# Weight addresses held in TensorE registers, and the batch order found by matmuls, in an attention and mixture-of-experts kernel

## The chip, the cores and the metric

The kernel runs on one core of a Trainium2 chip. The metric is the device time of one launch in microseconds, the median of several runs; lower is better. The profile is of one execution and counts from the start of its span.

## The reference

Two stages follow each other. The first is attention between 512 tokens x and 32 state rows, for 8 batches of 8 heads of width 64, in both directions:

```
scores = x @ state.T / 8 ;  xread = softmax(scores) @ state      # 512 rows a batch
scores2 = state @ x.T / 8 ; sread = softmax(scores2) @ x         # 32 rows a batch
rows = concatenate([xread, sread]) with the heads side by side   # 8 * 544 = 4352 rows of 512
```

The second is a mixture of 8 experts without dropping. Each row goes to the expert with the largest of its eight logits:

```
logits = rows @ w_gate ;  e = argmax(logits) ;  gate = softmax(logits)[e]
y = gate * (relu(rows @ w1[e]) @ w2[e])          # w1: 512 x 1024, w2: 1024 x 512, per expert
```

## The kernel before

**One expert a batch.** The kernel guesses the expert of each batch from the sums of its state rows, and lets all 512 token rows of the batch go through that one expert. The 256 state rows (32 a batch) are routed one batch at a time: each group of 32 rows has its own guess. At the end a flag says whether every row's true argmax was the guessed one; if not, a slow path under `tc.If` computes again. With the inputs of this study it isn't entered.

**Weights in slots.** The weights of all experts have a place in SBUF, `wt`, 8 slots of 16,384 fp16 values a partition: half 0 of a slot is w1, half 1 is w2. GpSimd loads them (`load_w`, with a cast from fp32 on the way), in the order in which the batches first need their expert: slot 0 is the expert of batch 0, and so on. Until they are loaded, parts of slots 6 and 7 serve as scratch and as two of the three buffers for x. So which slot a batch uses is known at run time only. The batch order is worked out on VectorE, on one partition (`guess_first` for batch 0, `guess_rest`, `guess_rest2` and `full_order` for the others), and leaves the loads' order in `ordi` and a word with three bits per batch in `slotw`. TensorE loads that word into a register (`slot_of`, line 437) and takes the batch's three bits (`field`, line 427).

**The letters.** The order on every engine is written out by hand, as strings of short names that `run` executes in turn. The ones used below, per batch: C casts x to fp16, T and X transpose it; N gives the scores `sn`, E, I and J their exponentials in two fp16 halves; S and F the scores the other way; G the gate logits, R, U, V, P and A the normalised attention `aT`; Z, z, t and u the state rows' reading into `sx`; M, g and h the gate. The token rows never become a 512 x 512 matrix: W multiplies the state by w1 (`sw`, copied to `SW` by K), L multiplies `SW` by `aT` (`hps`), H applies relu into `hT`, Q multiplies by w2 (`yps`, eight matmuls for each of four row groups), Y scales by the gate and O stores. Batch k's L, H, Q and Y run between the steps of batch k+1's attention (prefix `+`) and batch k+2's loading (`++`). `STEP` is the pattern of batches 3 to 6, `LATE` that of the first three.

**W.** For each of two halves fh of the hidden width, W issues eight matmuls of 64 rows by 32 columns, in eight places of the array (`pinned`, line 230), into two banks. K copies one bank each to `SW`. Three banks (`psm`) are shared by W, L and the tail's `hs`.

**The tail.** After the last batch the state rows of all batches are computed. s0 to s9 find their experts, in two groups g of 4 batches: each of the 32-row blocks j has a slot of its own, and the rows that don't agree with their block's main expert go through a third pass, p = 2, with a side (which of the groups) for each block. Pass p is l (`hs`: 32 matmuls of 128x32, four side by side), m (relu), n and o (transposes), q (`ys`, 32 matmuls) and y (scaling). v compares all token rows' choices with the guesses, w sums that into the flag with a matmul, r stores. The tail's order, at the end of the string for the last batch:

```
Q0 Y0a s3 s4 s5 s6 s7 s8 s9
l20 m20a l21 m21v Q1 Y1v O0
n2 o2v l00 m00a l01 m01a v w
q2 y2a n0 o0v
Q2 Y2a l10 m10a l11 m11v
q0 y0a r0 n1 o1v
Q3 Y3a O1
q1 y1a r1
```

s6 (line 594) loads two words into TensorE registers and takes sixteen fields out of them. Every matmul that reads `wt` at a run-time slot is written with a dynamic slice; the address is then computed by a register instruction ahead of each of these matmuls.

Of the kernel before, what the change touches and what calls it, by code (L numbers as in the profile page):

```python
# [19 lines left out]
B = 8  # L20
# [9 lines left out]
FAR = 1.0e6  # L30


def _consts():
# [3 lines left out]
        "bone": p[:, None] // 32 == np.arange(4)[None],  # L37
        "rev": np.broadcast_to(8 - np.arange(E), (128, E)),
        "pw": np.broadcast_to(2.0 ** (8 - np.arange(B)), (128, B)),
        "io": np.broadcast_to(np.arange(8), (128, 8)),  # L40
        "oct": np.broadcast_to(8.0 ** np.arange(B), (128, B)),
# [11 lines left out]
    )  # L53
    c = {
# [16 lines left out]
def kernel(  # L71
# [53 lines left out]
    posv = sb([1, E], FP32, "posv")  # L125
    hone = sb([1, B, E], FP32, "hone")
    ordi = sb([1, E + 1], I32, "ordi")
    slotw = sb([1, 1], I32, "slotw")
    vrow = sb([1, 2, E], FP16, "vrow")
# [13 lines left out]
    bone, rev, pw, io, octw = (const(1, n) for n in ("bone", "rev", "pw", "io", "oct"))  # L143
# [25 lines left out]
    zm = scr(256).rearrange("p (b e c) -> p b e c", b=B, e=E)  # L169
    zz = scr(64)  # L170
    hv = scr(256)
# [33 lines left out]
    def load_w(i, half, at=None):  # L205
        if ("w", i) not in order:
            at = i if at is None else at
            order["w", i] = P_.value_load(
                ordi[:, at : at + 1], min_val=0, max_val=E - 1
            )  # L210
        rv = order["w", i]
        if half == 0:
            s = moe_w1[ds(rv, 1)].rearrange("o (c l) f -> l (o c) f", l=128)
        else:
            s = moe_w2[ds(rv, 1)].rearrange("o (c l r) f -> l (o c) (r f)", l=128, r=2)
        ins = P_.dma_start(  # L216
            out=wt[:, i, half].rearrange("p (c f) -> p c f", c=4), in_=s
        ).ins
        tc.declare_no_dep(ins, group="wmm", reason="readers of slots filled before")
        tc.add_to_no_dep_group("w", ins)  # L220
        wloads[half].append(ins)
# [8 lines left out]
    def pinned(out, lhsT, rhs, pos, size, start, stop):  # L230
        def sym(ap, **k):
# [3 lines left out]

        name = (
# [7 lines left out]
            ins=[sym(rhs), sym(lhsT, for_matmul_weights=True)],  # L244
# [182 lines left out]
    def field(word, shift, mask):  # L427
        t = nc.tensor
        r = t.alloc_register(f"fld{len(order)}")
        order["fld", len(order)] = r  # L430
        if shift:
            t.reg_alu(r, word, shift, OP.logical_shift_right)
            t.reg_alu(r, r, mask, OP.bitwise_and)
        else:
            t.reg_alu(r, word, mask, OP.bitwise_and)
        return t.snap(r, min_val=0, max_val=mask)

    def slot_of(d):
        if "slot" not in d:
            if d["b"] == 0:  # L440
                d["slot"] = 0
            else:
# [4 lines left out]
                d["slot"] = field(order["word"], 3 * d["b"], 7)  # L447
        return d["slot"]

    def op_W(d, fh):  # L450
        slot = slot_of(d)
        d["sw", fh] = [bank([128, 512], FP32, "sw", psm) for _ in range(2)]
        for c in range(4):
            for r in range(2):
                rows = slice(64 * r, 64 * r + 64)
                i = pinned(
                    d["sw", fh][r][32 * c : 32 * c + 32],
                    d["bd"][rows, c, 32 * r : 32 * r + 32],
                    w1(slot, rows, c, fh * 512, fh * 512 + 512),
# [3 lines left out]
                    True,  # L463
                )
                if "loop" not in d and d["b"]:
                    first = fh == 0 and c == 0
# [25 lines left out]
    def op_Q(d, q):  # L492
        slot = slot_of(d)
        ps = d["yp", q] = bank([128, 512], FP32, "yps", psy)
        for f in range(8):
            i = mm(
                ps, hT[:, f, q * 128 : q * 128 + 128], w2(slot, f), f == 0, f == 7
            ).ins
            if "loop" not in d and d["b"]:
                dyn(i, wloads[1][: d["b"] + 1] if q == 0 and f == 0 else ())  # L500
# [93 lines left out]
    def op_s6(_):  # L594
        w = [
            nc.tensor.value_load(g_["swi"][:, k : k + 1], min_val=0, max_val=m)
            for k, m in ((0, 2**24 - 1), (1, 2**24 - 1))
        ]
        g_["slots"] = [
            [field(w[0], 12 * g + 3 * j, 7) for j in range(4)] for g in range(2)  # L600
        ] + [[field(w[1], 5 * j, 7) for j in range(4)]]
        g_["side"] = [field(w[1], 5 * j + 3, 1) for j in range(4)]
# [52 lines left out]
    def lhs_state(p, j, c, t=0):  # L655
        if p < 2:
            return sx[:, t, c, p, j, :]
        return sx[:, t, c, ds(g_["side"][j], 1), j, :].rearrange("p o n -> p (o n)")

    def op_l(_, p, fh):  # L660
        ps = g_["hs", p, fh] = bank([128, 512], FP32, "hs", psm)
        for c in range(4):
            for j in range(4):
# [3 lines left out]
                    w1(g_["slots"][p][j], slice(0, 128), c, fh * 512, fh * 512 + 512),  # L667
# [3 lines left out]
                    c == 3,  # L671
                )
                dyn(i, wloads[0] if c == 0 and fh == 0 and j == 0 else ())
# [23 lines left out]
    def op_q(_, p):  # L697
        ps = g_["ys", p] = bank([128, 512], FP32, "ys", psy)
        for f in range(8):
            for j in range(4):  # L700
# [3 lines left out]
                    w2(g_["slots"][p][j], f),  # L704
# [3 lines left out]
                    f == 7,  # L708
                )
                dyn(i, wloads[1] if f == 0 and j == 0 else ())  # L710

    def op_y(_, p, e):
        if p == 2:
            yS = g_["yS"] = sb([128, 2, DM], FP32, "ysb", 3)
            sd = g_["sdm"] = sb([128, 2], FP32, "sdm")
            V_.tensor_copy(sd, g_["gm"][:, 1])
            for g in range(2):
                scale(e, yS[:, g], g_["ys", 2], sd[:, g : g + 1])
            return
        if "yM" not in g_:  # L720
            g_["yM"] = sb([128, 2, DM], FP32, "ysb", 3)
        V_.scalar_tensor_tensor(
            g_["yM"][:, p],
            g_["ys", p],
            g_["gm"][:, 0, p : p + 1],
            g_["yS"][:, p],
            op0=OP.mult,
            op1=OP.add,
        )
# [10 lines left out]
    def run(table, k=0, ctx_=None):  # L740
        for w in table.split():
# [15 lines left out]
            elif n in "svwlmnoqyr" or n[0] == "s":  # L757
# [22 lines left out]
    A_.dma_start(kt[1][0], kt[1][1])  # L780
    state_first(nc.sync, 0)
    state_first(nc.sync, 1)
    A_.dma_start(wgr, moe_w_gate.rearrange("(c r) e -> r c e", r=128))
    A_.dma_start(kt[0][0], kt[0][1])
    load_x(0, nc.sync, 0, 4)
    load_x(0, nc.sync, 4, 8)
    for c in range(4):
        for r in range(2):
            state_dma(nc.sync, c, r)
    A_.dma_start(kt[2][0], kt[2][1])  # L790

    V_.memset(ones, 1.0)
    V_.memset(one32, 1.0)
    V_.memset(hT[:, 0], 0.0)
    scratch(V_.memset(wgx, 0.0))
    warm = sb([1, 1], FP32, "warm")
    V_.memset(warm, 0.0)
    A_.activation(warm, warm, AF.Exp)
    P_.memset(bd[:, 0], 0.0)
    P_.memset(bd[:, 1:B], 0.0)  # L800

# [44 lines left out]
    hrow = lambda k: hv[0:1, 64 * k : 64 * k + 64].rearrange("p (b e) -> p b e", e=E)  # L846
    mrow, krow = hv[0:1, 192:200], hv[0:1, 200:208]
    m8 = sb([1, 8], FP32, "m8")
    i8 = sb([1, 8], U32, "i8")

    def guess_first():
# [7 lines left out]
        h0 = sb([1, E], FP32, "h0")  # L859
        V_.tensor_copy(h0, hp)  # L860
        V_.max(m8, h0)
        V_.max_index(i8, m8, h0)
        V_.tensor_copy(ordi[:, E : E + 1], i8[:, 0:1])
        f0 = sb([1, 1], FP32, "f0")
        V_.tensor_copy(f0, i8[:, 0:1])
        V_.tensor_scalar(hone[:, 0], io[0:1], f0, None, op0=OP.is_equal)

    def guess_rest():
        sp = bank([128, 7, 4], FP32, "sp")
        for b in range(1, B):  # L870
            mm(sp[:, b - 1], stl[:, b, :], bone)
        wv = bc(wgr.rearrange("p c e -> p e c"), 1, 7)
        scratch(V_.tensor_tensor(zm[:, 1:B], bc(sp, 2, E), wv, op=OP.mult))
        scratch(V_.reduce_sum(zz[:, 8:64].rearrange("p (b e) -> p b e", e=E), zm[:, 1:B], axis=AX_X))

    def guess_rest2():
        hp = bank([1, 7, E], FP32, "hp7")
        mm(hp.rearrange("p b e -> p (b e)"), one32, zz[:, 8:64])
        h0 = hrow(0)[:, 1:B]
        mx = mrow[:, 1:B]  # L880
        scratch(V_.reduce_max(mx, hp, axis=AX_X))
        scratch(V_.tensor_tensor(h0, hp, bc(mx, 2, E), op=OP.is_equal))
        scratch(V_.tensor_tensor(h0, h0, bc(rev[0:1], 1, 7), op=OP.mult))
        scratch(V_.reduce_max(mx, h0, axis=AX_X))
        V_.tensor_tensor(hone[:, 1:B], bc(rev[0:1], 1, 7), bc(mx, 2, E), op=OP.is_equal)

    def full_order():
        h0, h1 = hrow(0), hrow(1)
        key = krow
        scratch(V_.tensor_tensor(h0, hone, bc(pw[0:1], 2, E), op=OP.mult))  # L890
        scratch(V_.reduce_sum(key, h0.rearrange("p b e -> p e b"), axis=AX_X))
        scratch(
            V_.scalar_tensor_tensor(key, key, 16.0, rev[0:1], op0=OP.mult, op1=OP.add)
        )
        scratch(V_.tensor_tensor(h1, bc(key, 1, E), bc(key, 2, E), op=OP.is_gt))
        V_.reduce_sum(posv, h1, axis=AX_X)
        scratch(
            V_.tensor_tensor(h0, bc(posv, 1, E), bc(io[0:1], 2, E), op=OP.is_equal)
        )
        scratch(V_.tensor_tensor(h0, h0, bc(io[0:1], 1, E), op=OP.mult))  # L900
        with nc.allow_low_precision(reason="small whole numbers"):
            V_.reduce_sum(ordi[:, 0:E], h0, axis=AX_X)

    def slot_word():
        h0, h1 = hrow(0), hrow(1)
        scratch(V_.tensor_tensor(h1, hone, bc(posv, 1, B), op=OP.mult))
        scratch(V_.tensor_tensor(h0, h1, bc(octw[0:1], 2, E), op=OP.mult))
        with nc.allow_low_precision(reason="whole numbers below 2 to the 24"):
            V_.reduce_sum(slotw, h0.rearrange("p b e -> p (b e)"), axis=AX_X)

    def codes():
        h0 = hrow(0)
# [243 lines left out]
```

## Time and profile before

| | |
|---|---|
| median of three runs | 225.24 us (222.94 to 226.63) |
| span of the profiled execution | 219.3 us |
| TensorE busy | 188.3 us, 86% |
| VectorE, ScalarE, GpSimd busy | 116.9, 87.0, 33.6 us |
| token matmuls `yps`, 256 | 60.0 us, 379 ns each as recorded, overlapping |
| state matmuls `hs` and `ys`, 96 each | 8% and 6% of the chain that ended last |
| `sw`, 128 | 8% of that chain |
| weight loads, 16 | 1024 KB each, 20.4 us from issue to landing (median) |

The page's busy share is an average over four stretches with different limits: the start until W of batch 0 (22.6 us), the way to W of batch 1 (54.4), six steps until W of batch 7 (157.7), and the tail. [...] so the pace is read from the distance of starts.

### The profile page before, as it was taken

Reading aid. Unit: us, or ns where it says so; the run is one execution under the profiler, and the core shown is the slowest. Engines: PE = TensorE matmul, PEld = TensorE weight load, DVE = VectorE, ACT = ScalarE, POOL = GpSimd, SP = SyncE. Lnnn points to the kernel's source line nnn. Section 1 sums busy time; section 2 is a strip of 40 time slices with the busy share of each in tenths; the row PEclk is TensorE's granted clock in tenths of the full one; section 3 lists DMA queues with packets and bytes.
Section 4 is the critical chain, followed back from the end, with each engine's and each line's share of the span. In section 5 each row is a group of like instructions: output and inputs, shape, how many; then the busy total and the mean of one; then the engine's idle time right before and its main releaser. Section 6 shows DMA issues by size and latency. Waiting matters only on the chain.

```text
span 219.3 us, 5315 instructions
## 1 busy us (share of the span) xinstructions
PE 188.3 (86%) x1934; PEld 99.2 (45%) x1935; DVE 116.9 (53%) x307; ACT 87.0 (40%) x170; POOL 33.6 (15%) x42
## 2 busy tenths in 40 slices
PE   5654767879999899899999999999997099999990
PEld 2244334545445445435545555554543022565650
DVE  1655466987578378476566566567567200611211
ACT  3260337604462571564475467368162101114010
POOL 3501000914300710460130022100000000000000
PEclk9996788999999999999999999999999979999997
DMA  5999800799999999999999955892202000200042
GB/s 112 233 229 274 256 5 0 119 211 275 290 205 298 263 250 295 257 279 275 253 221 247 302 199 92 204 185 99 100 13 83 0 3 0 84 17 0 3 144 57
DMA packets 17268, 35.26 MB, mean 161 GB/s; under 512 B 3800, under 2 KB 4952, under 8 KB 17240
## 3 DMA queue, kind: packets, MB, share of 16 engines
q0 software_dynamic: 10352, 24.12, 51.2%
q1 hardware_dynamic: 5736, 10.23, 13.6%
q10 hardware_dynamic: 1152, 0.53, 1.0%
q8 instruction: 19, 0.31, 0.6%
q14 instruction: 9, 0.07, 0.1%
HBM read 42.73 MB, written 8.91 MB: 236 GB/s over the span
## 4 chain that ended last, share of the span: by engine, by line
PE 78%; DVE 10%; ACT 4%; issue 3%; DMA 1%; SPq 0%; DVEq 0%; ACTq 0%
PE yps L86 25%; PE hps L86 13%; PE hs L252 8%; PE sw L252 8%; PE ys L252 6%; PE sr L86 4%; PE xtp L282 2%; PE lgp L86 2%; PE wp L86 1%; ACT xT L97 1%; PE sn L86 1%; DVE enlo L310 1%; PE ss L86 1%; DMA wt<-in_state_dram 1%; PE gp L86 1%
## 5 line engine op out<-in xcount | busy, mean ns | idle before, releaser
L86 PE MATMUL yps<-wt,hT 128*128 (+1 forms) x256 | 60.0, 379 | 0.0
L86 PEld LDWEIGHTS <-hT 128*128 128x128 f16 x256 | 24.2, 99 | 26.1 <-issue 1.6
L86 PE MATMUL hps<-aT,SW 128*128 128x512 f16 x128 | 33.2, 393 | 3.0 <-DVE hT L487 3.0
L504 ACT ACTIVATE ysb<-yps,gall 128x512 f32<-128x512 f32 x21 | 14.4, 687 | 31.8 <-PE yps L86 31.4
L487 DVE TENSOR_SCALAR hT<-hps 128x512 f16<-128x512 f32 x34 | 22.8, 689 | 7.2 <-PE hps L86 7.2
L252 PE MATMUL hs<-wt,sx 128*32 x96 | 18.5, 395 | 5.4 <-issue 5.2
L485 ACT ACTIVATE hT<-hps 128x512 f16<-128x512 f32 x30 | 17.8, 597 | 9.7 <-PE hps L86 9.1
L252 PE MATMUL sw<-wt,bd 64*32 (+1 forms) x128 | 19.1, 404 | 2.4 <-ACT SW L97 2.2
L86 PEld LDWEIGHTS <-SW 128*128 128x128 f16 x128 | 11.8, 99 | 19.5 <-issue 9.7
L97 ACT CAST SW<-sw 128x512 f16<-128x512 f32 x20 | 11.3, 588 | 21.0 <-PE sw L252 21.0
L216 POOL DMA_DIRECT2D wt<-in_moe_w_dram x16 | 12.2, 766 | 33.5 <-DVE sx L423 20.0
L252 PEld LDWEIGHTS <-sx 128*32 128x32 f16 (+1 forms) x96 | 6.8, 94 | 16.3 <-issue 14.4
L364 DVE TENSOR_TENSOR aT<-en,rcb 128x512 f16<-128x512 f32 x16 | 10.3, 684 | 6.0 <-PE rcb L86 5.9
L252 PEld LDWEIGHTS <-bd 64*32 64x32 f16 x128 | 8.0, 90 | 9.6 <-issue 5.2
L506 DVE TENSOR_SCALAR ysb<-yps,gall 128x512 f32<-128x512 f32 x11 | 8.2, 748 | 7.6 <-PE yps L86 7.6
L97 DVE CAST SW<-sw 128x512 f16<-128x512 f32 x12 | 8.3, 690 | 7.2 <-PE sw L252 7.0
L310 DVE TENSOR_TENSOR enlo<-en,enhi 128x512 f16<-128x512 f32 x16 | 10.6, 690 | 2.8 <-ACT enhi L97 2.5
L97 DVE COPY xT<-xtp 128x1024 f16<-128x1024 f16 x8 | 5.5, 692 | 10.9 <-PE xtp L282 10.8
L302 ACT ACTIVATE en<-sn 128x512 f32<-128x512 f32 x16 | 9.4, 593 | 3.8 <-PE sn L86 3.8
L485 ACT ACTIVATE enlo<-hs 128x512 f16<-128x512 f32 x3 | 1.8, 597 | 20.9 <-PE hs L252 20.9
L97 POOL CAST xhi<-wt 128x1024 f16<-128x1024 f32 x8 | 8.3, 1072 | 9.7 <-DMA wt<-in_x_dram 5.4
L282 PE MATMUL xtp<-pack,xhi 128*128 128x128 f16 x128 | 8.5, 219 | 1.2 <-DVE sx L422 1.2
(175 smaller groups left out, 239.7 us busy)
## 6 DMA issues: line engine op xcount, KB each, us to landing
wt<-in_moe_w_dram POOLq DMA_DIRECT2D x16, 1024.0 KB, 20.4
out_dram<-ysb SPq DMA_DIRECT2D x16, 512.0 KB, 6.9
wt<-in_x_dram POOLq DMA_DIRECT2D x4, 1024.0 KB, 16.4
x32c<-in_x_dram POOLq DMA_DIRECT2D x3, 1024.0 KB, 22.7
wt<-in_x_dram SPq DMA_DIRECT2D x2, 512.0 KB, 6.2
wt<-in_state_dram SPq DMA_DIRECT2D x8, 56.0 KB, 6.0
out_dram<-ysb SPq DMA_DIRECT2D x4, 64.0 KB, 2.1
out_dram<-ysb ACTq DMA_DIRECT2D x4, 64.0 KB, 2.7
```

Source lines behind the costliest of these rows:

```text
L86: return nc.tensor.matmul(out, lhsT=lhsT, rhs=rhs, start=start, stop=stop, skip_group_check=True)
L97: return {"a": A_.copy, "v": V_.tensor_copy, "p": P_.tensor_copy}[e](o, i)
L216: ins = P_.dma_start(out=wt[:, i, half].rearrange("p (c f) -> p c f", c=4), in_=s).ins
L252: i = nc.tensor.add_instruction(ins)
L282: nc.tensor.transpose(tp[:, c, q, :], xhi[:, q, o : o + 128], id16)
L302: A_.activation(en[:, r], d["sn"][r], AF.Exp, scale=0.125, accum_out=d["rz"][:, r : r + 1])
L310: {"v": V_, "p": P_}[e].tensor_tensor(d["enlo"][:, r], en[:, r], d["enhi"][:, r], op=OP.subtract)
L364: V_.tensor_tensor(d["aT"][:, r], en[:, r], d["rcb"][r].rearrange("p q s -> p (q s)"), op=OP.mult,)
L485: A_.activation(o, i, AF.Relu)
L487: V_.tensor_scalar(o, i, 0.0, None, op0=OP.max)
L504: A_.activation(o, i, AF.Copy, scale=g)
L506: V_.tensor_scalar(o, i, g, None, op0=OP.mult)
```

## The change

It has four parts, all meant to leave TensorE less to wait for.

- **Addresses in registers.** `slot_base` computes a batch's byte address in `wt` once, `at_reg` adds the offsets, and `held` gives a matmul its address straight from a register. The operations f (fifteen addresses for W) and a (eight for Q) are put in the order ahead of their use; only the first matmul of each group keeps the dynamic slice, and with it the wait for the load. In the tail b gives twelve slot bases, and c gives two sets (a, b) of eight addresses, the next one while the present one is used.
- **The tail's order.** Passes run 0, 1, 2 rather than 2, 0, 1, Q1 lies ahead of the slot bases, y of pass 2 adds onto the other two, m of the second halves is on VectorE, and v and w stand behind pass 1. e touches slot 7 with two small matmuls.
- **The order by matmuls, early.** The guess for batches 1 to 7 uses eight partitions and small matmuls (`guess_1` to `guess_4`), between the L of batch 0; Z, M, g, h and the block layout of the state (`set_bd`) move behind L. `max` and `max_index` read PSUM, and the first expert's index is taken from `i8` directly.
- **x first.** x of batch 0 is the first on SyncE's queue; the state goes on ScalarE's, the constants on GpSimd's, `bone` is made by memsets, and the loads of the remaining state are split over two queues. One half of slot 7 is loaded a batch earlier.

```diff
@@ start
+    load_x(0, nc.sync, 0, 4)
+    load_x(0, nc.sync, 4, 8)
+    state_first(A_, 0)
+    state_first(A_, 1)
     A_.dma_start(wgr, moe_w_gate.rearrange("(c r) e -> r c e", r=128))
-    A_.dma_start(kt[0][0], kt[0][1])
-    load_x(0, nc.sync, 0, 4)
-    load_x(0, nc.sync, 4, 8)
-    for c in range(4):
-        for r in range(2):
-            state_dma(nc.sync, c, r)
-    A_.dma_start(kt[2][0], kt[2][1])
+    P_.dma_start(kt[0][0], kt[0][1])
+    P_.dma_start(kt[1][0], kt[1][1])
...
+    for c in range(4):
+        for r in range(2):
+            state_dma((nc.sync, A_)[r], c, r)
+    nc.sync.dma_start(kt[2][0], kt[2][1])
@@ addresses
+    def slot_base(name, word, shift):
+        t, r = nc.tensor, reg(name)
+        if shift:
+            t.reg_alu(r, word, shift, OP.logical_shift_right)
+        t.reg_alu(r, r if shift else word, 7, OP.bitwise_and)
+        t.reg_alu(r, r, 2 * 2 * 4096, OP.mult)
+        t.reg_alu(r, r, WT_AT, OP.add)
+        return r
+
+    def at_reg(name, base, el, row=0):
+        nc.tensor.reg_alu(reg(name), base, 2 * el + (row << 18), OP.add)
...
+    def op_c(_, p, k):
+        o = "ab"[k % 2]
+        for i in range(2):
+            for j in range(4):
+                n = 2 * (k % 4) + i
+                el = (n % 4) * F + n // 4 * 512 if k < 4 else 4096 + n * 512
+                at_reg(f"s{o}{i}{j}", regs[f"b{p}{j}"], el)
@@ op_W
-                    w1(slot, rows, c, fh * 512, fh * 512 + 512),
+                    w1(0 if held_ else slot, rows, c, fh * 512, fh * 512 + 512),
                     (64 * r, 32 * c),
                     (64, 32),
                     True,
                     True,
+                    f"f{fh}{c}{r}" if held_ else None,
@@ op_l
-                    w1(g_["slots"][p][j], slice(0, 128), c, fh * 512, fh * 512 + 512),
+                    w1(0, slice(0, 128), c, fh * 512, fh * 512 + 512),
...
+                    f"s{'ab'[k % 2]}{c % 2}{j}",
...
+                if c % 2 == 0 and j == 3 and k < 3:
+                    op_c(None, p, k + 1)
@@ STEP
-Q2 Y2a
+Q2 +f Y2a
 +U +Va +Z +z +W0 +K00a +K01a +P +A0 +A1 +W1 +K10a +K11v +t +g +u
@@ batch 0
+    guess_1()
+    run("L0 H0a L1 H1a", 0)
+    guess_2()
+    run("L2 H2a L3 H3a", 0)
+    guess_3()
     run("L4 H4a L5 H5a", 0)
-    guess_rest2()
-    run("L6 H6a L7 H7a +C0v +C1a", 0)
-    turn_state(1, 5, lambda b: stl[:, b, :], "a")
-    turn_state(5, 8, lambda b: stl[:, b, :], "a")
-    full_order()
+    guess_4()
     load_w(1, 0)
     load_w(1, 1)
+    run("L6 H6v L7 H7a", 0)
+    run("M g Z z h", 0)
+    run("+C0v +C1a", 0)
+    set_bd(1, B, "av")
     run("t u +T0 +X0a +T1 +X1v", 0)
-    load_x(3)
+    turn_state(1, 5, lambda b: stl[:, b, :], "a")
+    turn_state(5, 8, lambda b: stl[:, b, :], "v")
     slot_word()
     set_gates(1, 8, "v")
+    load_x(3)
@@ tail
-s0 s1 s2
+s0 s1 s2 a
 Q0 Y0a s3 s4 s5 s6 s7 s8 s9
-l20 m20a l21 m21v Q1 Y1v O0
-n2 o2v l00 m00a l01 m01a v w
-q2 y2a n0 o0v
-Q2 Y2a l10 m10a l11 m11v
-q0 y0a r0 n1 o1v
-Q3 Y3a O1
-q1 y1a r1
+Q1 b0 b1 b2 c00 Y1v O0
+l00 m00a l01 m01v
+Q2 Y2a n0 o0v c10
+e l10 m10a l11 m11v v w c04 q0 y0a
+n1 o1v c20 l20 m20a l21 m21v c14 q1 y1a
+Q3 Y3a O1 c24
+n2 o2v q2 y2a r0 r1
```

## The prediction

> **What bounds the kernel now.** I read busy time by stretch first, then the chain of waits, then the timeline of TensorE in one steady step and in the tail. The stretches (busy time of each engine, then the granted clock, the DMA share, GB/s):
>
> ```profile
> 0.00:22.63 22.63, 13.32 (x163) 8.05 (x165) 9.96 (x35) 6.42 (x13) 6.51 (x11) 0.90 0.97 212
> 22.63:54.38 31.75, 24.95 (x268) 14.28 (x265) 23.52 (x70) 13.75 (x26) 8.43 (x10) 0.91 0.61 139
> 54.38:157.69 103.31, 100.32 (x1180) 52.55 (x1180) 66.72 (x152) 56.20 (x113) 18.66 (x21) 1.00 0.95 231
> 157.69:219.30 61.61, 49.68 (x328) 24.32 (x328) 16.72 (x51) 10.67 (x19) 0.00 (x0) 0.95 0.11 36
> ```
>
> The steps between 54 and 158 us are TensorE-bound: 100.3 of 103.3 us, the vector and scalar engines far below. So whatever shortens TensorE there shortens the kernel, if the DMA (0.95) keeps up. In the tail nothing but TensorE works. Inside one step:
>
> ```profile
> 105.37 1.33 PE L252 MATMUL sw<-wt,bd 64*32 x8
> 106.63 0.40 PE L86 MATMUL rcb<-rcT,pack 32*128 32x128 f16 x8
> 106.95 1.42 PE L252 MATMUL sw<-wt,bd 64*32 x8
> ...
> 147.91 0.41 PE L86 MATMUL sn<-xT,bd 64*32 64x512 f16 x8
> ```
>
> `sw` and `sn` are the same matmul, eight of 64x32 with 512 columns, but `sw` reads expert weights at an address known at run time: 1.33 us against 0.41. The trace's records of TensorE's sequencer, which the page leaves out of busy time, say why: ahead of each `sw` matmul stands one fused register instruction of 55 ns, and the next of them starts 133 ns later. In the tail:
>
> ```profile
> 172.20 3.21 issue
> 175.41 3.47 PE hs L252 x9
> ...
> 187.25 1.83 PE yps L86 x8
> ...
> 189.46 3.45 PE L252 MATMUL hs<-wt,sx 128*32 x32
> 192.54 0.19 PE L86 MATMUL fp<-sfl,one 128*1 128x2 f32 x2
> ```
>
> 3.2 us go to decoding slots, and the first 32 `hs` matmuls take 11.8 us (175.4 to 187.2) with three register instructions each, where the next 32 take 3.45 with one. In the start two waits matter: matmuls held until the vector engine, busy with other work, empties a bank, and a long vector chain ahead of the second batch:
>
> ```profile
> 29.51 0.59 PE L86 MATMUL hps<-aT,SW 128*128 128x512 f16 x2 [3.00 <-DVE hT L487]
> 40.75 1.36 DVE L824 CAST gs_hi<-wt 128x448 f16<-128x448 f32 x1
> 42.14 1.34 DVE L825 TENSOR_TENSOR gs_lo<-wt,gs_hi 128x448 f16<-128x448 f32 x1
> ```
>
> [...] the first twelve `hs` of the pass at 189.46, whose register work was done beforehand, start in groups of four every 216 ns. [...] those twelve show that the sequencer does run ahead. It has a limit there: the third register instruction of the second `sw` group starts at 107.24, just when the second matmul, which waits for ScalarE, is let go. A waiting matmul so holds the register work behind it. [...] here `rcb` starts 0.305 us after the last `sw`. [...]
>
> **What is left of the issue cost.** A register instruction of 79 ns with nothing behind it is followed by the next 137 ns after its start, so one costs its duration plus 58. Then 133 - 55 - 58 leaves 20 ns for a matmul and its weight load. That is below the 54 ns that four side by side allow (216/4), so with addresses held, I take the array's pace: 32 packed matmuls in 1.8 us, eight `sw` starting within 0.15 us. The upper bound is 133 - 55 = 78 ns a pair.
>
> **Steps, part by part.** Batches 4 to 7: the first `sw` keeps its start (two register operations and a fused one stand ahead of it as before; the new ones, placed behind Q2, lie beside the 1.7 us of its matmuls). The eighth starts 0.8 us earlier, so does `rcb`. The second matmul of the next group still waits for the ScalarE copy of 0.59 us, which starts when the first group's row 0 is done: at 105.88 instead of 106.57, so that wait ends at 106.56 instead of 107.24. The remaining six need 0.15 instead of 0.77. `tt` starts at 106.98 instead of 108.31: 1.3 us x 4 = 5.3. Batches 2 and 3: that copy is behind the x copy on ScalarE (the chain runs ysb, xT, SW from 72.32 to 74.44), so only the second group gains, 0.95 x 2 = 1.9. Batch 1: 1.35. The 256 `yps` run at 216 ns, array-bound, with their register work hidden; they gain nothing. Taken off: the eight address operations now ahead of Q0 follow a matmul that waits, 0.3 us twice. Sum: 5.3 + 1.9 + 1.35 - 0.6 = 7.95.
>
> **Tail.** Decoding: the loads of two words and four side bits still stand between `wd` and Q1 (0.41 + 0.7 + 0.3, and four of 0.2: about 2.3 us), then Q1's 1.73 covers most of the twelve slot bases (12 x 0.204 = 2.45), so the first `hs` starts near 175.4 as before, but Q1 is already done; address operations ahead of Q0 add 0.35. From there: `hs` 0 1.8, Q2 1.8, transposes 0.55, `hs` 1 with the two touches 1.9, `ys` 0 1.8, 0.55, `hs` 2, `ys` 1 1.8, Q3 1.8, 0.55, a copy that nothing hides 1.0, `ys` 2 1.8. `hs` 2 keeps two fused instructions for its run-time side, 2 x 113 = 226 ns a matmul, with the address sets 8.0 us. New is a wait: `fp` (line 649 before) stands behind `hs` 1 and waits for the check v, five vector operations of 1.64 us busy, which are now queued behind the m copy of that same `hs` 1 (0.69). Before, m was on ScalarE and v ran beside the matmuls. `ys` 0 stands behind `fp` on TensorE, so 2.9 us of nothing. Sum 26.25. Then two combining operations of 0.75 instead of one, 1.8 with the semaphore, and the output as before (214.73 to 219.3: 4.55). 26.25 + 1.8 + 4.55 + 0.35 = 32.95 against 219.3 - 175.4 = 43.9: 10.95 gained.
>
> **Start.** x is the first on its queue. Before, its first half was issued at 2.27 and had landed at 7.4, so 5.1 us later, among four other loads; issued at 0.9, with fewer beside it, I estimate 5 us. `bone` by memset (six of 0.06 to 0.27 us) and the constants on GpSimd lie beside the load of the state, which ends near 4 us, and cost nothing. But ScalarE's third state load waits for that landing (a semaphore used again), behind it are queued a fourth issue, the st16 copy and the bd copy, and VectorE's own bd copy stands ahead of the x copy: 7.2 us. Two x copies of 1.03 and the transposes put `sn` at 10.6 instead of 13.03; the set_gates chain, now ahead of I0 on VectorE, gives part back (J1 ends 15.4, not 16.5). Z (1.94 us) moves out from ahead of W0, so W0 starts near 19 instead of 22.63; its weights landed at 16.7 and stay that early. H on ScalarE paces L at 0.6 us, with four guess steps between, and L ends at 27.5 instead of 35.2; w1 is issued at 28 instead of 38.4. But M, g, z, h, two casts of x, bd, u, X1 and the set_gates chain (3.4 us) then stand in one row on VectorE: `gp` starts at 35.2 instead of 38.42. With about 0.5 us of new address work before batch 1's first `sw`: 2.6 us gained. The bounds are 1 and 8 (the order known 10 us earlier, and that chain hidden).
>
> DMA: w2's first half landed at 63.3 and was used at 73; a batch's loads take about 15 us while the queue is full (94.2 to 109.6), a step 16.1 after the change. With w1 issued 10 us earlier it keeps ahead.
>
> **Sum.** 7.95 + 10.95 + 2.6 = 21.5 us, from the median 225.24: 203.7, taken as 203.5.
>
> **The rivals.**
> - The held matmuls still issue at 78 ns. For: that is the gap after the register instruction. Against: the 20 ns worked out above. Then 7 x 16 x 55 ns = 6.2 less 0.6 in the steps, and 5 x 0.7 less in the tail: 15.65 gained, 209.6.
> - The start gains 8 us, not 2.6: 198. For: 3 us of waiting for hT go, and the batch order comes early. Against: the vector chain above.
> - x first displaces the state and the gate matrix, the first expert and its load come late, and the start loses 3 instead: 209.
> - The other side: held matmuls lose their weight prefetch. 217 `yps` at 99 ns of exposed load are 21.5 us, with 300 packed ones more: 228 or slower. Against: `yps` runs at 216 ns with register addresses already.
>
> **Numbers.** Forecast 0.55, quick start 0.19, 78 ns 0.13, late start 0.08, lost prefetch 0.03, and 0.02 about unchanged. The range reaches from 196 (start at its upper bound and a tail 2 us better) to 210. Faster 0.95, same 0.02, slower 0.03.
>
> **What would show it.** Right: eight `sw` in about 0.45 us; `hs` and `ys` passes of 1.8 us but one of 8; TensorE idle for nearly 3 us at `fp`, released by the vector sum; `sn` near 10.6. Wrong: packed passes of 2.5 us; steps no shorter than 17 us, with waits for weights; a first order later than 6 us.

## The result, and the profile after

The changed kernel takes 208.24 us (median of 3 runs, 206.48 to 209.23) against 225.24 before. The ratio is 0.928, with a 95% interval of 0.910 to 0.947. That is faster, inside the range of the prediction, and 4.7 us above the predicted time. The two profiled executions differ by less (219.3 and 206.6 us, 12.7) than the medians (17.0), since the profiled one of before (222.11 us) was quicker than all three of its timed runs. Stage by stage, with the forecast of each stage worked out from the prediction's own terms:

| Stage | before | forecast | after |
|---|---|---|---|
| start to the first W (batch 0) | 22.63 | 19 | 21.98 |
| to W of batch 1 | 31.75 | 32.8 | 36.49 |
| W of batch 1 to the first `hs` | 121.03 | 113.4 | 113.61 |
| the first `hs` to the end | 43.89 | 32.6 | 34.52 |

So the steps, the core of the change, came as forecast to 0.2 us in sum. The start lost 4.1 us where 2.6 were to be gained, and the tail lost 1.9 us of its forecast gain. Between these two executions the forecast is missed by 8.8 us; that the medians show only 4.7 is owed mostly to the quick execution of before.

Here are the stretches again (busy time of TensorE, its weight loads, VectorE, ScalarE, GpSimd, each with its count; then granted clock, DMA share, GB/s), now cut where W of batches 0, 1 and 7 begin, to within 0.1 us:

```profile
0.00:21.98 21.98, 11.52 (x104) 6.33 (x107) 9.24 (x35) 6.58 (x14) 7.52 (x13) 0.89 0.78 181
21.98:58.47 36.49, 32.28 (x346) 19.68 (x346) 21.86 (x70) 14.54 (x26) 9.52 (x12) 0.74 0.92 202
58.47:155.10 96.63, 92.70 (x1187) 47.88 (x1186) 66.43 (x152) 55.58 (x112) 17.61 (x20) 1.00 0.94 224
155.10:206.60 51.50, 34.35 (x330) 15.64 (x330) 17.34 (x51) 10.18 (x18) 0.00 (x0) 0.92 0.13 43
```

The third and fourth lines are the gain: 96.6 us for 103.3, and still all TensorE, and 51.5 for 61.6. The second is the loss. Its granted clock is 0.74 where the same stretch had 0.91 before, and TensorE is busy 32.3 us of it where it was busy 25.0. The step that the prediction took apart now reads, in the timeline of TensorE:

```profile
107.32 0.41 PE L256 MATMUL sw<-wt,bd 64*32 x8
107.66 0.40 PE L93 MATMUL rcb<-rcT,pack 32*128 32x128 f16 x8
107.99 0.85 PE L256 MATMUL sw<-wt,bd 64*32 x8
```

Eight `sw` take 0.41 us for 1.33, which is what `sn` takes. In the third line 0.85 holds the wait for ScalarE's copy of SW, which stayed, as the prediction said.

The chain of waits in the start shows the failed part (start, duration, what):

```profile
0.89 4.18 DMA wt<-in_state_dram
5.08 3.20 DMA wt<-in_state_dram
8.28 0.56 PE sp L93 x2
...
10.29 0.71 DVE xhi L104
...
23.86 3.08 PE sp L93 x14
...
41.01 3.19 PE gp L93 x14
...
46.13 2.65 PE yps L93 x8
```

The state of batch 0, in two halves issued at 0.89 and 2.07, is what the first sum waits for, until 8.28; before, that sum began at 4.26. The first cast of x begins at 10.29 (before: 9.15), although x itself now lands early (its two halves took 4.6 us in the median from issue, for 6.2). So x first bought nothing: x waited for its turn on VectorE behind the state. Then the fp32 groups `sp` and `gp` take 3.1 and 3.2 us and the first Q 2.65. In the chain of before they read:

```profile
30.10 1.53 PE sp L86 x14
38.42 1.58 PE gp L86 x14
45.97 1.73 PE yps L86 x8
```

The timeline of TensorE in the tail:

```profile
180.90 0.19 PE L93 MATMUL fp<-sfl,one 128*1 128x2 f32 x2 [2.58 <-DVE sfl L709]
181.14 3.50 PE L256 MATMUL ys<-wt,es 128*32 x32
185.13 6.13 PE L256 MATMUL hs<-wt,sx 128*32 x32
191.14 1.99 PE L256 MATMUL ys<-wt,hts 128*32 x32
196.19 1.93 PE L256 MATMUL ys<-wt,es 128*32 x32 [0.78 <-DVE es L104]
```

The wait at `fp` is there with the forecast releaser. The `ys` behind it takes 3.5 us, not 1.8, and the pass with run-time sides 6.1, not 8. (Between the last `hs` and the first `ys` TensorE has 2.8 us with nothing but `fp`.)

### The profile page after: what moved, and what is told of

Same layout as the page of the kernel before. It is cut to its first block, busy times and chain, and to the rows that moved or that the text cites. A ratio compares the mean times of both kernels' runs of the same rounds, so it can differ in the third digit from the quotient of the medians.

```text
span 206.6 us, 4933 instructions
## 1 busy us (share of the span) xinstructions
PE 170.8 (83%) x1950; PEld 89.5 (43%) x1951; DVE 114.9 (56%) x307; ACT 86.9 (42%) x170; POOL 34.7 (17%) x44
## 4 chain that ended last, share of the span: by engine, by line
PE 74%; DVE 9%; ACT 6%; DMA 4%; issue 4%; DVEq 0%; ACTq 0%
PE yps L256 24%; PE hps L93 15%; PE hs L256 5%; PE yps L93 4%; DMA wt<-in_state_dram 4%; PE sr L93 4%; PE ys L256 4%; PE xtp L286 3%; PE sw L256 3%; ACT SW L104 3%; PE lgp L93 2%; PE ss L93 2%; PE gp L93 2%; PE sp L93 2%; PE sn L93 1%
## 5 line engine op out<-in xcount | busy, mean ns | idle before, releaser
L256 PE MATMUL yps<-wt,hT 128*128 x224 | 52.6, 379 | 3.2 <-DVE sfl L691 2.7
L256 PEld LDWEIGHTS <-hT 128*128 128x128 f16 x224 | 21.3, 99 | 26.9 <-issue 5.5
L529 DVE TENSOR_SCALAR hT<-hps 128x512 f16<-128x512 f32 x33 | 22.1, 689 | 6.9 <-PE hps L93 6.9
L527 ACT ACTIVATE hT<-hps 128x512 f16<-128x512 f32 x31 | 18.4, 598 | 11.6 <-PE hps L93 11.1
L104 ACT CAST SW<-sw 128x512 f16<-128x512 f32 x20 | 11.3, 588 | 7.3 <-PE sw L256 7.2
L256 PE MATMUL sw<-wt,bd 64*32 (+1 forms) x128 | 9.5, 412 | 3.3 <-ACT SW L104 2.3
L256 PE MATMUL hs<-wt,sx 128*32 x96 | 10.1, 380 | 1.1 <-issue 1.1
L286 PE MATMUL xtp<-pack,xhi 128*128 128x128 f16 x128 | 9.9, 236 | 1.4 <-DVE xhi L104 0.8
L286 PEld LDWEIGHTS <-xhi 128*128 128x128 f16 x128 | 8.6, 106 | 3.8 <-DVE xhi L104 2.0
L104 ACT COPY xT<-xtp 128x1024 f16<-128x1024 f16 x8 | 8.1, 1007 | 2.5 <-PE xtp L286 2.5
L327 ACT ACTIVATE es<-ss 128x512 f32<-128x512 f32 x16 | 8.7, 592 | 0.8 <-PE ss L93 0.8
```

Source lines behind the costliest of these rows:

```text
L104: return {"a": A_.copy, "v": V_.tensor_copy, "p": P_.tensor_copy}[e](o, i)
L256: i = nc.tensor.add_instruction(ins)
L286: nc.tensor.transpose(tp[:, c, q, :], xhi[:, q, o : o + 128], id16)
L327: A_.activation(d["es"][:, h * 2 : h * 2 + 2], d["ss", h], AF.Exp, scale=0.125)
L527: A_.activation(o, i, AF.Relu)
L529: V_.tensor_scalar(o, i, 0.0, None, op0=OP.max)
```

## The experiments

All of them start from one kernel, called base: the changed kernel, with two forms of matmul replaced. Ratios are against the kernel before, timed beside each on the same chip.

**base.** W's matmuls use all 128 rows; the sides of pass 2 are constants.

```diff
-                            at_reg(f"f{fh}{c}{r}", d["base"], c * F + fh * 512, 64 * r)
+                            at_reg(f"f{fh}{c}{r}", d["base"], c * F + fh * 512)
...
-                rows = slice(64 * r, 64 * r + 64)
+                rows = slice(0, 128)
...
-                    d["bd"][rows, c, 32 * r : 32 * r + 32],
+                    d["bd"][:, c, 32 * r : 32 * r + 32],
...
-                    (64 * r, 32 * c),
-                    (64, 32),
+                    (0, 32 * c),
+                    (128, 32),
...
-        return sx[:, 0, c, ds(g_["side", j], 1), j, :].rearrange("p o n -> p (o n)")
+        return sx[:, 0, c, (1, 0, 1, 0)[j], j, :]
```

> The changed kernel in a form that the next ones can be compared with. W's matmuls use 128 rows of the array, not 64 (the block layout of the state has zeros in the other half, so the sums are the same), still with run-time addresses held in registers; the four sides of pass 2 are written as constants (those of these inputs), which leaves out their choice at run time. Expected: W's eight matmuls in two groups of four after one another, 0.63 us for 0.41, some 0.4 us in each of seven batches (+2.6); the third hs pass 2 us for 6.05 (-4). Near 206.8 us. W of batch 1 starts at 58.5 us as in the changed kernel.

Measured: 207.38 us, ratio 0.928 (0.920 to 0.936), the same ratio as the changed kernel. Eight `sw` take 0.63 us and the step 16.29 for 15.90; the third `hs` pass takes 1.91 us for 6.13, as the other two do. So it is the two fused instructions for the side that made that pass long. W of batch 1 starts at 58.50: base shows the same start.

**state_first.** Was the late state the cause?

```diff
-    load_x(0, nc.sync, 0, 4)
-    load_x(0, nc.sync, 4, 8)
-    state_first(A_, 0)
-    state_first(A_, 1)
+    state_first(nc.sync, 0)
+    state_first(nc.sync, 1)
+    load_x(0, nc.sync, 0, 4)
+    load_x(0, nc.sync, 4, 8)
```

> Base, but the state of batch 0 is first on SyncE's queue again and x behind it, as before the change; all the rest as changed. If the late landing of the state lost the start (theory A), the first sum matmul starts near 4.3 us for 8.3, the first weights are issued near 7.8 for 11.5, sn starts near 11 for 13.2, and the kernel is 2 to 4 us faster than base. If the slow TensorE clock and the vector engine's row lose it (theory B), under 0.7 us is gained.

Measured: 206.53 us (0.914 to 0.934 of before, not to be told from base). `sp` starts at 5.74 rather than 8.21, W of batch 0 at 20.54 rather than 21.85, but W of batch 1 at 58.88. The 1.3 us are gone before they reach the loop. Theory A falls as the whole cause, though the edit brought back only part of the lateness (5.74, where the kernel before had 4.26). Part of the loss on the way is clock: between the two W the clock record of this execution shows half speed for 21.2 us, that of base for 18.9. ScalarE shows why little came even of the early state: it issues half of the other state loads, and that issue held it to 8.2 us (4.50 from 3.73), ahead of its copy of the state at 8.27.

**warm.** Is it the clock?

```diff
     run("C0v T0 X0a C1v T1 X1v N", 0)
+    spare(7)
...
-    run("G R U Va P A0 A1", 0)
+    run("G R", 0)
+    spare(4)
+    run("U Va", 0)
+    spare(1)
+    run("P A0 A1", 0)
...
-    run("t u +T0 +X0a +T1 +X1v", 0)
+    spare(3)
+    run("t u", 0)
+    spare(3)
+    run("+T0 +X0a", 0)
+    spare(1)
+    run("+T1 +X1v", 0)
...
+    spare(3)
     slot_word()
```

> Base with 22 more matmuls on data that nobody reads, put into TensorE's idle time between 14 and 41 us; they only keep it busy. Theory B (the idle time lets the granted clock fall to half): the sums sp and gp take 1.6 us each for 3.2, the first Q 1.8 for 2.8, and W of batch 1 starts 3 to 5 us earlier. Theory A (only the late state): the clock returns, but the vector and scalar engines set the pace anyway, and under 1 us is gained.

Measured: 201.50 us, ratio 0.903 (0.893 to 0.912). The stretch 38 to 48 us in base, and then in warm:

```profile
38.00:48.00 10.00, 9.01 (x59) 6.81 (x59) 5.47 (x15) 4.01 (x9) 3.22 (x4) 0.52 1.11 239
```

```profile
38.00:48.00 10.00, 8.93 (x94) 5.59 (x91) 7.62 (x21) 3.74 (x9) 2.90 (x4) 1.00 1.11 247
```

The clock is 1.00 for 0.52, and 94 matmuls were done in it, not 59. `gp` takes 1.77 us for 3.25 and the first Q 1.89 for 2.52; `sp` got back only half of its loss (2.23 for 3.15). From W of batch 0 to W of batch 1 it is 33.35 us, for 36.65; in the seven other variants of base without the fillers (state_first, v_early, x_early, new_tail and the three dyn runs) it lay between 36.0 and 38.3. So theory B holds: 3.3 us of that stretch were clock. W of batch 0 itself came 0.3 us later. The two profiled executions differ by 6.2 us, and most of the rest looks like chance: 1.3 us lie behind the last `ys`, in the output, which the fillers don't touch, and 1.6 in `ys` 0, behind the same pause of 2.58. In base, and then in warm:

```profile
183.76 0.19 PE L93 MATMUL fp<-sfl,one 128*1 128x2 f32 x2 [2.58 <-DVE sfl L709]
184.01 3.56 PE L256 MATMUL ys<-wt,es 128*32 x32
```

```profile
180.64 1.95 PE L256 MATMUL ys<-wt,es 128*32 x32
```

Equal pauses, one followed by slow matmuls and one not. In these two executions the recorded clock changes at times that lie 3.41 us or a multiple of it apart (in the kernel before: 175.02 and 178.43). Counted on from the recorded changes before the pause (170.45 in base, 171.84 in warm), such times are 180.70 and 184.11 in base and 178.67 in warm. In base the whole pause fell between 180.70 and 184.11, a stretch in which TensorE worked 0.8 us, and the clock dropped to 0.50 at 184.11; in warm 178.67 split the pause, and it didn't drop. A split alone doesn't decide it: in state_first 181.67, counted in the same way, split the same pause, and the clock dropped at 185.08. What decides it is not shown.

**v_early.** The wait at `fp`.

```diff
-l00 m00a l01 m01v
+l00 m00a l01 m01v v
...
-e l10 m10a l11 m11v v w c04 q0 y0a
+e l10 m10a l11 m11v w c04 q0 y0a
```

> Base with the vector engine's check v one line of the tail's order earlier, behind the second half of pass 0, where it lies beside Q2; fp stays where it is. If the wait at fp is only that row, the idle time ahead of fp (2.8 us in the changed kernel) goes, and if the slow ys 0 (3.5 us) is the clock after that pause, ys 0 falls to 1.8: together 4.3 us faster than base. If something else holds ys 0 (its register addresses), 2.8 us.

Measured: 202.06 us, ratio 0.904 (0.891 to 0.917). The timeline of TensorE:

```profile
179.97 0.17 PE L93 MATMUL fp<-sfl,one 128*1 128x2 f32 x1
...
180.02 1.89 PE L256 MATMUL ys<-wt,es 128*32 x29
```

No idle time is put down at `fp` any more, and `ys` 0 has its 1.9 us. Between the first `hs` and the last `ys` base took 19.77 us and this kernel 15.04: 4.7 us for one letter of the order, 3.0 of them ahead of `ys` 0 (the pause) and 1.6 in it (the clock, recorded as 1.00 here and as 0.50 from 184.11 in base). Register addresses hold nothing back there.

**combo_1.** The three edits above at once.

> Base with three edits together: the state first on SyncE, the 22 idle-filling matmuls, and v one line earlier. Alone against base they measured -0.9, -5.9 and -5.3 us. If the state's late landing only hid behind the slow clock, it now counts, and the sum is more than its parts: 193 to 195. If the start is set by the vector engine's row in any case, 196 to 197.

Measured: 198.18 us, ratio 0.884 (0.878 to 0.891): slower than either expectation, and than the sum of the three gains (195.3). That sum counts the 1.6 us of `ys` 0 twice if the other runs of warm were like its profiled one: they were chance in warm, and v_early brings them too. Without them it is 196.9. The profile shows one loss: the idle-filling matmuls themselves, `wp` in the timeline.

```profile
13.97 3.15 PE L93 MATMUL wp<-hT,ones 128*128 128x512 f16 x7
...
24.90 1.46 PE L256 MATMUL sw<-wt,bd 128*32 128x512 f16 x9
```

Seven of them took 3.15 us, one every 0.43 us; in warm the same seven took 1.98, the later ones one every 0.21. At 0.43 us each they no longer fit into the idle time and push the transposes behind them: W of batch 0 starts at 24.90, 3 us later than in base. But this is one execution, at 200.9 us the slowest of the five; the others took 197.1 to 198.8. Whether they lost the same is not shown, and what makes the remaining 1.3 us is open.

**x_early.** The consumers of x ahead of the guess.

```diff
     spare(6)
+    run("C0v T0 X0a C1v T1 X1v", 0)
     guess_first()
...
-    run("C0v T0 X0a C1v T1 X1v N", 0)
+    run("N", 0)
```

> Base with the casts, transposes and copies of x of batch 0 ahead of the first guess in every engine's order, so that x, which lands first, is also used first. If x first was lost because its consumers stood behind the state on the vector engine, sn starts near 10.5 us for 13.1 and W of batch 0 near 20 (the landing of its weights) for 21.8. What is gained by then is kept to W of batch 1 (1.5 to 2 us) if the clock holds, and mostly lost before it (under 0.7) if the matmuls after it still run at half clock.

Measured, one run: 206.78 us. `sn` starts at 11.55 for 13.12, W of batch 0 at 20.98 for 21.85, W of batch 1 at 58.25 for 58.50. The place in VectorE's order is worth 0.9 us by W of batch 0 and 0.25 by W of batch 1: lost again on the way, as in state_first. The edit had a price as well: the first guess now stands behind the work on x, and the first weights are issued at 12.12 for 11.40.

**dyn_w, dyn_w1.** The held addresses of W undone: the slot once as an expression, and once decoded into a register first, as in the kernel before (the second part of the diff is in dyn_w1 alone).

```diff
-                held_ = "loop" not in d and d["b"] and not first
+                held_ = "loop" not in d and d["b"] and not first and False
...
-                d["slot"] = (order["word"] >> (3 * d["b"])) & 7
+                r = reg("slot_w")
+                nc.tensor.reg_alu(r, order["word"], 3 * d["b"], OP.logical_shift_right)
+                nc.tensor.reg_alu(r, r, 7, OP.bitwise_and)
+                d["slot"] = nc.tensor.snap(r, min_val=0, max_val=7)
```

> Base with the addresses of all W matmuls as dynamic slices again, one fused register instruction ahead of each. If that instruction sets the pace (133 ns a matmul in the kernel before), a group of eight takes 1.1 to 1.3 us for 0.63, and a step 0.8 to 1.0 us more: 5 us slower than base. If the array sets it, nothing changes.

> As dyn_w (W with dynamic slices), but with the slot decoded into a register first, as in the kernel before: one fused instruction a matmul. dyn_w left the slot as an expression, and its eight took 2.5 to 2.8 us. If the number of register instructions sets the pace, eight now take 1.1 to 1.4 us, a step 0.8 to 1.2 us more than base, and the kernel 5 to 7 us more (near 213).

The same group of W of batch 4 in base, in dyn_w1 and in dyn_w:

```profile
108.17 0.63 PE L256 MATMUL sw<-wt,bd 128*32 x8
```

```profile
110.23 1.30 PE L256 MATMUL sw<-wt,bd 128*32 x8
```

```profile
116.11 2.83 PE L256 MATMUL sw<-wt,bd 128*32 x8
```

One run each: 210.91 us for dyn_w1 and 226.27 for dyn_w. The step, from W to W of batches 5 and 6, is 16.29 us in base, 17.34 in dyn_w1 and 19.91 in dyn_w. So the number of register instructions ahead of each matmul sets the pace, and one of them costs 1.05 us a step in these late batches even where the array needs 0.63 us for the group. By W of batch 7 dyn_w1 is 5.1 us behind base (162.1 for 157.0), of which 0.8 were there at W of batch 1 already: 4.3 us in six steps. Only 3.5 are left at the end (near 213 was expected), in part since its first Q of the tail ran at full clock (1.89 us for 3.34). An expression as the slot made three instructions of one, which the expectation of dyn_w had not seen: the trace has two plain and one fused ahead of each of these eight matmuls, so the dynamic slice computes its expression anew at each use.

**dyn_s.** The same undone in the tail's packed passes.

```diff
-                    w1(0, slice(0, 128), c, fh * 512, fh * 512 + 512),
+                    w1(g_["slots"][p][j], slice(0, 128), c, fh * 512, fh * 512 + 512),
-                    w2(0, f),
+                    w2(g_["slots"][p][j], f),
```

with twelve slots decoded into registers in `op_s6`, and b and c empty.

> Base with the addresses of the tail's packed passes hs and ys as dynamic slices of slots held as small numbers. If register work sets their pace, passes with one such instruction a matmul take 3.45 us for 1.9 and those in which the sequencer meets a slot for the first time up to 11.8, as in the kernel before: 12 to 20 us slower than base. If the array sets it: no slower.

Measured, one run: 222.34 us, 15 more than base. From the timeline of TensorE:

```profile
175.92 3.57 PE L256 MATMUL yps<-wt,hT 128*128 x8 [4.22 <-issue]
...
207.43 4.69 PE L256 MATMUL ys<-wt,es 128*32 x32 [0.88 <-DVE es L104]
```

4.22 us go to decoding before Q1, `ys` passes take 4.7 us for 1.9, and `hs` 2.9 to 3.9. No pass came near 11.8, the upper end of the expectation, which had the wrong reason for that length. In the kernel before, that pass had three register instructions ahead of each matmul, two of them for the run-time side, which is a constant here:

```profile
175.41 11.83 PE L252 MATMUL hs<-wt,sx 128*32 x32 [5.21 <-issue]
```

These matmuls start 370 ns apart; those of dyn_w, with three as well, 351; with the two for the side alone, in the changed kernel, 226 (185 over the whole pass, since its first eleven start faster); with one, in dyn_w1, 133.

**new_tail.** Nothing is left out here; the sides are chosen at run time.

```diff
-Q0 Y0a s3 s4 s5 s6 s7 s8 s9
-Q1 b0 b1 b2 c00 Y1v O0
-l00 m00a l01 m01v
-Q2 Y2a n0 o0v c10
-e l10 m10a l11 m11v v w c04 q0 y0a
-n1 o1v c20 l20 m20a l21 m21v c14 q1 y1a
-Q3 Y3a O1 c24
-n2 o2v q2 y2a r0 r1
+Q0 Y0a s3 s4 s5 s7 s8 s9
+Q1 s6 b0 Y1v O0
+Q2 c00 Y2a
+l00 m00a l01 m01v v
+Q3 b1 c10 Y3a O1 n0 o0v
+e l10 m10a l11 m11v w c04 q0 y0a
+b2 c20 n1 o1v l20 m20a l21 m21v c14 q1 y1a
+n2 o2v c24 q2 y2a r0 r1
@@ batches 1 to 3
-Q2 Y2a +u +h
+Q2 +f Y2a +u +h
...
-        run("+f +W0 +K00a +K01v +W1 +K10a +K11v", k)
+        run("+W0 +K00a +K01v +W1 +K10a +K11v", k)
@@ op_s6
+            P_.tensor_copy(
+                g_["s2"][:, :, j, :],
+                sx[:, 0, :, ds(side, 1), j, :].rearrange("p c o n -> p (c o) n"),
+            )
```

> Base, with nothing left out, and the tail put in another order: Q1 ahead of the loads of the slot words, Q2 ahead of the first hs, v behind the second half of pass 0, Q3 where Q2 was; the sides of pass 2 are chosen at run time by four copies on GpSimd with run-time addresses; the fifteen addresses of W of batches 1 to 3 are computed two Q earlier. If decoding and the wait at fp were what the tail lost: 4.7 us from v and 2 from the decoding under Q1 and Q2, 1.2 at W of batches 1 to 3: 199 to 200. If GpSimd's copies come too late for pass 2, a wait shows ahead of its hs, and 1 to 3 us of it are lost.

Measured: 198.41 us, ratio 0.889 (0.880 to 0.898). No wait shows ahead of the third `hs`. From W of batch 7 to the last `ys` it is 30.4 us; it was 32.7 in v_early. The 1.2 us expected at W of batches 1 to 3 didn't come: W of batch 1 starts 0.4 us earlier, and the steps of batches 1 to 3 take what they took in base (17.99, 18.01 and 13.70 us).

**new_start.** new_tail with the start rearranged, and with more idle-filling matmuls than the expectation names: three more in the start (`spare`) and four in the tail, ahead of the expert counts:

```diff
-    load_x(0, nc.sync, 0, 4)
-    load_x(0, nc.sync, 4, 8)
-    state_first(A_, 0)
+    state_first(nc.sync, 0)
     state_first(A_, 1)
+    load_x(0, nc.sync, 0, 4)
+    load_x(0, nc.sync, 4, 8)
...
-            state_dma((nc.sync, A_)[r], c, r)
+            state_dma(nc.sync, c, r)
...
+    turn_state(0, 1, lambda b: st0[:, 0, :], "v")
+    set_gates(0, 1, "v")
+    spare(4)
+    run("C0v T0 X0a C1v T1 X1v N E0 S0 I0v E1 J0v S1 I1a J1v", 0)
+    guess_hot()
...
+    guess_1()
+    run("F0 F1 G R", 0)
+    spare(2)
+    run("U Va", 0)
+    guess_2()
+    run("P A0 A1", 0)
+    run("W0 K00a K01v W1 K10a K11v", 0)
+    guess_3()
+    run("M g", 0)
+    run("L0 H0a L1 H1a", 0)
+    guess_4()
...
+    run("L2 H2a L3 H3v", 0)
+    set_bd(1, B, "av")
+    run("L4 H4a L5 H5v +C0v L6 H6a +C1a L7 H7v", 0)
@@ guess_1
-        sp = bank([128, 4, 7], FP32, "sp7")
+        sp = bank([128, 4, 7], FP32, "sp7", psm)
@@ op_s2
+        wq = bank([128, 512], FP32, "wq")
+        for _i in range(4):
+            mm(wq, ones, hT[:, 0])
```

> new_tail with another start: one half of the first state at the head of each hardware queue, x behind it, the other state loads all on SyncE; gates of batch 0 ahead of the casts of x; the sums for the order ahead of G, the rest of the guess between R and L; M beside L, the block layout and the casts of x of batch 1 between the L. If the start was lost to state that came late and to rows on the vector engine that batch 1 waits for, W of batch 0 starts near 17 us for 21.9, the second weights are issued near 23 for 33, W of batch 1 starts near 50 for 58.5, and the kernel takes 190 to 193. If the half clock takes it back, W of batch 1 starts after 54 and the kernel takes 196 or more.

Measured: 189.57 us, ratio 0.849 (0.840 to 0.858), the fastest of all. W of batch 1 starts at 50.12, as expected, but by another way: W of batch 0 starts at 21.70, not 17, and the second weights are issued at 28.85, not 23. Nearly the whole gain lies between W of batch 0 and W of batch 1: 28.4 us for 36.24 in new_tail. How much of it is the order and how much the clock is not separated: the granted clock of that stretch is 0.93 for 0.73, the fillers are part of the edit, and no run leaves them out. The chain of waits tells what held W of batch 0:

```profile
2.08 6.05 DMA wgr<-in_moe_w_gate_dram
8.27 0.36 PE hp L93 x8
```

The state is used at 4.01 now, and the gate matrix, 16 KB, has taken the state's place as the late one.

**gate_first.** One line moved.

```diff
     state_first(nc.sync, 0)
+    A_.dma_start(wgr, moe_w_gate.rearrange("(c r) e -> r c e", r=128))
     state_first(A_, 1)
...
-    A_.dma_start(wgr, moe_w_gate.rearrange("(c r) e -> r c e", r=128))
```

> new_start with one edit: the gate matrix (16 KB, but 512 pieces of 32 bytes) is issued ahead of the second half of the first state on ScalarE, not behind it. In new_start it was issued at 2.08 us, beside x, and landed 6.05 us later; the first hp waited for it to 8.27. If what is issued beside x comes late whatever its size, hp now starts near 5 us, the first weights are issued near 7 for 10.65, sn starts near 11 for 14.5, W of batch 0 near 18.5 for 21.7, and up to 3 us reach the end: 186.5 to 188. If batch 1 waits for other things by then (its x, the vector engine), W of batch 1 stays at 50 and the time near 189.5. If the second half of the state now comes late instead, hp starts as late as before.

Measured: 191.04 us, ratio 0.854 (0.848 to 0.860): none of the expected gain; the interval overlaps that of new_start. `hp` starts at 6.12 for 8.27, the first weights are issued at 8.50 for 10.65, `sn` starts at 12.31. And then, in the timeline of TensorE:

```profile
17.30 3.12 PE L93 MATMUL sp<-bone,wt 128*128 128x4 f32 x14 [2.56 <-DMA wt<-in_state_dram]
...
23.67 1.46 PE L256 MATMUL sw<-wt,bd 128*32 128x512 f16 x9
```

The first expert's megabytes, issued 2 us earlier, ran beside the state of the other batches. The last piece of that state was issued at 9.35, now behind these weights, and landed at 16.85; in new_start it was issued at 9.55, ahead of them, and landed at 11.43. The sums for the order, which need it, stand ahead of G. TensorE fell to about half its pace meanwhile (`sp` 3.12 us for 1.70 in new_start). W of batch 0 starts 2 us later than in new_start, and W of batch 1 3.3 us later (53.43).

## Why the prediction was right in the steps and wrong in the start

- **Steps (forecast 7.95 gained).** Right in mechanism and in the sum. To the first `hs` the forecast was 113.4 us and 113.6 came. That it is so close is in part luck: the steps of batches 4 to 6 gained 1.5 us each for 1.3, those of batches 1 to 3 together 2.1 for 2.65. The rival of 78 ns a matmul is out: eight `sw` take 0.41 us. dyn_w1 puts one fused instruction back, and the step grows by 1.05 us.
- **Start (forecast 2.6 gained; 4.1 lost).** This is the term that failed, by 6.7 of the 8.8 us. Two of its steps were wrong. First, "the constants ... lie beside the load of the state, which ends near 4 us": it ended at 8.28, beside x. With the copies that stand behind it this put `sn` at 13.2 for 10.6 and W of batch 0 at 21.98 for 19, 3.0 us. The sign named for it, a first order later than 6 us, came: the first expert is known at 9.9. The rival "x first displaces the state and the gate matrix" had named this, and its time, 209, is close to what came, though by chance: it knew nothing of the second step. Undoing the displacement alone gives back 1.3 us at W of batch 0 and nothing later, since each early load made another one late (state, ScalarE's queue, gate matrix, the rest of the state; state_first, new_start, gate_first). How the 3.0 us divide among them stays open. Second, the stretch to W of batch 1, forecast at 32.8 us, took 36.5. The prediction put the clock of the start at nothing: it names none there, and in the kernel before `sp`, `gp` and the first Q had run at a recorded 1.00 (1.53, 1.58 and 1.73 us). warm gives 3.3 of those 3.7 us back by keeping TensorE busy, with no other change.
- **Tail (forecast 11.3 gained from the first `hs` on, 9.4 came; the 10.95 of the sum has 0.35 of address work ahead of it taken off).** The pause at `fp` was 2.8 us for a forecast of 2.9, with the right cause. "Nothing but TensorE works" in the tail was too strong: VectorE works 16.7 of its 61.6 us, and the check v is part of that. Two terms were mis-sized and cancel by luck: `ys` 0 took 3.5 us for 1.8, as the clock fell at the end of that pause (recorded as 0.50 from 180.99 to 184.41), and v_early, without the pause, has 1.9; the `hs` with run-time sides took 6.1 for 8.0. Counted from the first `hs` to the end of the last `ys`, 26.07 us came for 26.25. What is left is the output: "as before (4.55)", but 6.96 came from the end of the last combining operation. Before, half of the stores had been issued earlier; now all eight wait for the last pass, four on each queue. Their issue takes 2.5 us for 1.69 with two, but it begins after the first of the two combining operations and ends 1.9 us after the second, for 1.7 before. Most of the difference is in the landing of the last store of each queue: 4.1 and 4.2 us from issue, where those of before took 2.8 and 3.0. It varies: in runs with this same output, 7.0 us (dyn_w) to 8.8 us (base) pass from the last `ys` to the end, 8.5 in the changed kernel. No run tested the order of the stores.
- **DMA.** No wait of TensorE for the weights shows in the loop, as forecast.

## What to carry to other kernels

Keep register work off the path of small matmuls: compute addresses ahead and hold them, and decode an expression once, since each dynamic slice pays for it again (a group of eight `sw` took 0.63 us with held addresses, 1.30 with one register instruction ahead of each, 2.83 with three). Here each move of one load to the head of a queue made some other small load the last, and brought little where its consumer was not next on its engine (in state_first 1.3 us at W of batch 0 and nothing at W of batch 1); follow the chain of waits after each such move. Ask of TensorE's work in a stage with idle gaps what it would take at half clock (`gp` 3.2 us for 1.6 here), and of a pause whether it costs its own length alone or that of slow matmuls behind it as well (2.8 and 1.7 us in the changed kernel).

## What the runs showed of the hardware that was not expected

- A granted clock of 1.00 in the first microseconds can mean that there is no record. The trace of the changed kernel has its first clock record at 13.74 us, that of before at 11.18, and the clock column shows 1.00 for what lies ahead. Three matmuls of 512 columns at 9.44 start 0.43 us apart there and take 1.49 us, as the same three do in warm at a recorded 0.50; so the first stretches, 0.90 before and 0.89 after, ran in part at a lower clock than that. Where there is a record, durations agree with it: in warm the distance falls from 0.40 to 0.21 us at 14.9, and the record changes at 14.83:

```profile
14.20 1.98 PE L93 MATMUL wp<-hT,ones 128*128 128x512 f16 x7
```
- Loads in small pieces came late beside a large one on another queue. The two loads of the first state, 32 KB each in pieces of 256 bytes, needed from 0.89 to 8.13 us in the changed kernel beside 1 MB of x; in new_start, both at the head of their queues, they had landed at 3.9. The 16 KB of gate matrix in pieces of 32 bytes needed 6.05 us beside x (new_start) and 2.0 us ahead of it (gate_first).
- Small VectorE operations took several times their usual length beside a GpSimd that issued loads or cast: the first one-hot row 1.00 us in the changed kernel, 0.22 in combo_1, where GpSimd had finished, and in x_early, where it had not yet begun; the two copies of the gate matrix 0.57 and 0.96 for 0.16 and 0.18 in both. That is seen side by side, not tested.
